# Gated attention and a SiLU layer on one core: the fourth pair's first product in plain fp32, spare tiles for the first chunks, a new order

## The chip, the cores and the metric

The kernel runs on one core of one Trainium2 chip. The core has a matmul engine (PE, with its weight loads listed apart as PEld), a vector engine (DVE), an activation engine (ACT), GpSimd (POOL) and SyncE (SP); the last two serve here mostly to issue DMAs. The metric is the device time of one execution in microseconds (us). Before the change the median of 3 runs was 649.08 us (647.99 to 651.11).

## The reference

The program computes a gated linear attention step by step over 768 positions, for 4 batches and 8 heads of 48 channels, and passes its output through a two-matrix layer with a SiLU between. `x` has 3072 rows (tokens) of 384 values, `w_in` is 384 x 2048, `w_out` 2048 x 384.

```
mag = sqrt(a_re^2 + a_im^2);  scale = min(mag, 0.999) / (mag + 1e-6)
for t in range(768):
    S_re, S_im = (ar*S_re - ai*S_im + k_t v_t^T,  ar*S_im + ai*S_re)
    y[t] = q_t . S_re
x = y as (3072, 384)
h = x @ w_in;   g = h * sigmoid(h);   out = g @ w_out
```

## The kernel before, in words

**Tiling.** The 3072 tokens are cut into 24 chunks of 128, and two chunks make a pair of 256 tokens (12 pairs, 0 to 11). For a chunk `n` the attention part turns the gates into log decays (`l`, tile `s1`) and angles (`th`), sums them along the chunk with a matmul (`L`, `phase`), takes exponentials and sines (`eq`, `ek`, `cs`), multiplies them into q and k (`qr`, `kr`), transposes these (`T`), forms the weights of the chunk (`a`, masked into `w`), and multiplies by v and by the carried state (`y`). The pair's output stands transposed in `xT`.

**The layer.** For a pair `p` and a step `jp` of 0 to 7 (256 hidden columns each), `hidden` (token `h:p.jp`) makes the first product into a PSUM tile `h`, `silu` (`g:p.jp`) applies the activation, and `result` (`r:p.jp`) adds the second product into `o`. There are two PSUM tiles for `h`.

**Plain and in parts.** A product is either plain (fp32 operands, line 755: 6 products of 128x128 by 128x256 for a step, which the trace shows as 12 matmuls) or in parts (fp32r operands, line 762: three forms, coarse, fine and diff, 18 matmuls for a step). Which pair does what is in the table `IN_PARTS`: pairs 0 to 2 are plain, 3 to 11 in parts. The parts of x are `xH` (ACT), `xL` and `xD` (DVE), two tiles of each, used by odd and even pairs in turn. The parts of `w_in` are made once, for each of the eight steps, by `v_head` (ACT, line 796), `v_tail` (DVE, 800), `v_scaled` (ACT, 804) and `v_placed` (ACT, 810), which overwrites the plain weights in place, so it has to follow the last plain product of those columns. The fine part is written to DRAM (`vk`) and read back for each use (`lv`) into a ring of three tiles that the second product's `diff` loads share; `v_mixed` (`vx`, DVE) makes the third form from it, once for pair 3 and from pair 4 on once for two pairs. The second product is in parts from pair 2 on.

**What sets the order.** The program is a list of some 1900 tokens; each issues one such step on its engines, and each engine works through its instructions in that order. Tiles are taken from rings, so a step also waits until the tile's former reader is done. DMAs are issued from SP and POOL (the token's letter `g` means POOL), from ACT for the output. Tokens `warm:n` are `n` matmuls without use.

Of the kernel before, what the change touches and what calls it, by code (L numbers as in the profile page):

```python
# [70 lines left out]
def kernel(  # L71
# [985 lines left out]
    with tc.manual_schedule():  # L1057
        for x in """
                re:0 im:0 e0:0 e1:0 warm:30 e2:0 im:1 e4:0 re:1g e0:1 e6:0 e7:0 e1:1 e2:1 warm:34
                e3:0 e5:0 re:2g e8:0 e4:1 e6:1 im:2g L:0 e3:1 exp:0 im:3g q:0g e5:1 e7:1 at:0.0  # L1060
                re:3g e8:1 an:0.0 at:0.1 k:0g L:1 dk:0 an:0.1 phase:0 G0:1 phase:1 k:1g rd:0 dq:0
                v:0g rd:1 turn:0 q:1g trig:0 turn:1 trig:1 F: G5:1 warm:20 F: rq:0.0 exp:1 rk:0.0
                hold: last:0 G8:1 rq:0.1 rk:0.1 t:0.2 H: v:1g G1:1 k:2g t:0.3 sm:0 G7:1 q:2g T:0.3
                dq:1 dk:1 t:0.0 T:0.2 s:0 rq:1.1 G2:1 t:0.1 rk:1.1 ends:0 T:0.0 t:1.3 w:0.0 F:
                rq:1.0 G3:1 T:1.3 H: G4:1 T:0.1 G6:1 G9:1 lk:0 L:2 t:1.1 exp:2 rk:1.0 w:0.1 m:0.0
                v:2g R: m:0.1 L:3 Ga:1 S:0 thirds:0 T:1.1 s:1 phase:2 ends:1 re:4g J: q:3g sm:1
                exp:3 lk:1 dq:2 rd:2 k:3g turn:2 trig:2 S:1 H: w:1.1 F: t:1.0 t:1.2 dk:2 rk:2.0
                T:1.0 rk:2.1 T:1.2 y:0 last:2 t:2.0 R: im:4g T:2.0 thirds:2 x:0 m:1.1 w:1.0 F:
                phase:3 H: R: F: thirds:1 m:1.0 rd:3 turn:3 re:5g rq:2.0 trig:3 t:2.1 rq:2.1 y:1 R:
                im:5g J: x:1 t:2.2 J: R: R: dk:3 G0:2 J: s:2 t:2.3 h:0.1 H: H: dq:3 ends:2 last:1  # L1070
                T:2.2 rq:3.1 rk:3.1 rk:3.0 F: v:3g rq:3.0 T:2.1 J: h:0.0 H: R: G5:2 w:2.0 S:2 t:3.0
                t:3.2 k:4g m:2.0 T:2.3 g:0.1 t:3.1 J: T:3.0 T:3.2 g:0.0 q:4g w:2.1 m:2.1 J: t:3.3
                w:3.0 G1:2 ends:3 last:3 y:2 m:3.0 F: G7:2 T:3.1 H: T:3.3 F: r:0.0 w:3.1 x:2 F: H:
                R: G3:2 thirds:3 R: G6:2 F: F: J: G8:2 G2:2 m:3.1 r:0.1 k:5g G9:2 y:3 H: R: H: R:
                F: im:6g v:4g F: x:3 s:3 J: Ga:2 R: H: h:1.0 J: R: h:1.1 sm:2 F: im:7g F: carried:5
                H: G4:2 L:4 g:1.0 carried:4 J: S:3 r:1.0 h:1.2 H: g:1.1 J: r:1.1 exp:4 g:1.2 F: R:
                phase:4 R: H: F: ends:4 lk:2 h:0.2 J: re:6g J: rd:4 h:0.3 R: R: turn:4 H: trig:4
                last:4 H: dq:4 r:1.2 F: F: re:7g F: phase:5 g:0.2 J: R: J: R: Q:4 h:1.3 dk:4 H:
                rd:5 J: K:4 turn:5 g:0.3 R: H: L:5 H: J: R: F: g:1.3 exp:5 J: R: r:0.2 G0:3 q:5g F:
                H: F: s:4 H: v:5g J: H: r:1.3 R: tk:4 h:1.4 g:1.4 ends:5 F: J: R: trig:5 J: F: F:  # L1080
                h:0.4 h:0.5 tq:4 H: dk:5 F: J: G5:3 g:0.4 H: G1:3 G7:3 r:0.3 J: r:1.4 R: G8:3 h:1.5
                dq:5 g:0.5 R: Q:5 H: td:4 r:0.4 G3:3 H: J: S:4 R: R: K:5 r:0.5 G2:3 H: w:4.1 J: J:
                J: tk:5 tq:5 g:1.5 G4:3 G6:3 q:6g w:4.0 wq:0 G9:3 k:6g m:4.1 wd:0 h:0.6 q:7g ws:0
                v:6g wq:1 td:5 im:8g Ga:3 m:4.0 wd:1 wq:3 g:0.6 L:6 wk:0 ws:1 wq:7 wd:3 exp:6 h:0.7
                wq:2 we:0 y:4 wq:4 r:0.6 wq:5 carried:6 dk:6 x:4 wd:2 carried:7 g:0.7 ws:2 w:5.0
                m:5.0 v:7g wk:1 re:8g last:5 wq:6 ends:6 w:5.1 ws:3 we:1 m:5.1 phase:6 rd:6 dq:6
                wd:5 im:9g we:3 h:1.6 k:7g turn:6 y:5 L:7 r:1.5 wk:2 wd:4 we:5 wk:3 ws:5 we:2 g:1.6
                trig:6 ws:4 x:5 s:5 q:8 Q:6 k:8 wd:7 S:5 re:9g K:6 xd:2 wk:5 r:1.6 we:4 ws:7 exp:7
                tk:6 tq:6 vh:1 h:1.7 h:2.0 wk:4 wd:6 we:7 last:6 g:1.7 phase:7 v:8 h:2.1 wk:7 vh:0
                rd:7 g:2.0 vt:1 vt:0 gr:2.0 r:1.7 vs:1 vs:0 r:0.7 turn:7 td:6 vp:0 w:6.0 vp:1 vk:1  # L1090
                of:1 gb:2.0 G0:4 w:6.1 ws:6 m:6.0 we:6 g:2.1 m:6.1 of:0 vk:0 G5:4 dk:7 G1:4 y:6
                lw:2.1 s:6 wk:6 G2:4 gc:2.0 G7:4 G3:4 G8:4 ends:7 h:2.2 G4:4 dq:7 lw:2.0 G6:4 r:2.0
                gr:2.1 k:9 lw:2.2 h:2.4 ss:6 vh:2 q:9 G9:4 g:2.2 sm:3 gb:2.1 gc:2.1 Ga:4 r:2.1 vt:2
                x:6 gr:2.2 v:9 vh:3 trig:7 lk:3 sd:6 gb:2.2 vt:3 gc:2.2 vs:2 re:10 h:2.3 r:2.2 hl:8
                last:7 ul:8 g:2.3 L:8 g:2.4 h:2.5 vs:3 Q:7 K:7 im:10 carried:8 exp:8 ht:8 tk:7 vk:2
                tq:7 h:2.6 ut:8 lw:2.3 gr:2.3 im:11 gb:2.3 gc:2.3 vp:2 g:2.5 phase:8 vk:3 ends:8
                lw:2.4 vh:5 vp:3 vt:5 td:7 r:2.3 gr:2.4 vh:4 hl:9 gb:2.4 vt:4 g:2.6 dk:8 rd:8 h:2.7
                s:7 vp:4 re:11 vp:5 vs:5 vh:7 dq:8 vh:6 ul:9 turn:8 S:6 gc:2.4 r:2.4 vk:5 ss:7
                last:8 carried:9 vs:4 w:7.1 vt:7 trig:8 q:10 gr:2.5 w:7.0 vt:6 vs:7 g:2.7 vk:4 K:8
                vs:6 m:7.1 L:9 Q:8 exp:9 vk:7 vp:6 m:7.0 tk:8 ht:9 dk:9 vk:6 vp:7 ut:9 lw:2.5 tq:8  # L1100
                G0:5 y:7 ends:9 gb:2.5 G5:5 gc:2.5 x:7 phase:9 r:2.5 G1:5 k:11 lw:2.6 gr:2.6 s:8
                rd:9 v:10 G8:5 G7:5 G3:5 turn:9 dq:9 gb:2.6 ss:8 G6:5 gc:2.6 G9:5 lw:2.7 r:2.6 xd:3
                Ga:5 trig:9 gr:2.7 gb:2.7 carried:10 xh:3 lv:3.0 gc:2.7 k:10 td:8 r:2.7 G2:5 xt:3
                ht:10 xg:3 vx:3.0 ut:10 G4:5 h:3.0 g:3.0 lv:3.1 im:12 phase:10 vx:3.1 hl:10 ul:10
                h:3.1 gr:3.0 gb:3.0 L:10 carried:11 sd:7 lw:3.0 g:3.1 ht:11 lv:3.2 last:9 gc:3.0
                im:13 re:12 rd:10 r:3.0 K:9 lv:3.3 Q:9 turn:10 gr:3.1 vx:3.2 re:13 gb:3.1 ut:11
                w:8.0 exp:10 m:8.0 last:10 h:3.2 phase:11 tk:9 trig:10 rd:11 tq:9 ends:10 w:8.1
                vx:3.3 dq:10 Q:10 hl:11 q:11 lw:3.1 ul:11 turn:11 lv:3.4 td:9 gc:3.1 S:7 G0:6 dk:10
                h:3.3 r:3.1 m:8.1 s:9 g:3.2 sd:8 G5:6 g:3.3 vx:3.4 ss:9 last:11 K:10 y:8 gr:3.2
                lw:3.2 gb:3.2 L:11 G1:6 tk:10 x:8 h:3.4 lv:3.5 exp:11 tq:10 lv:3.6 ends:11 gc:3.2  # L1110
                G7:6 w:9.0 r:3.2 m:9.0 G2:6 gr:3.3 vx:3.5 G3:6 G4:6 w:9.1 v:11 dk:11 m:9.1 h:3.5
                td:10 trig:11 G6:6 g:3.4 lw:3.3 dq:11 G8:6 s:10 gb:3.3 G9:6 hl:12 y:9 vx:3.6 x:9
                ss:10 gc:3.3 h:3.6 r:3.3 K:11 sd:9 gr:3.4 Q:11 w:10.1 Ga:6 tk:11 w:10.0 g:3.6 ul:12
                g:3.5 lw:3.4 gb:3.4 gc:3.4 tq:11 sm:5 m:10.1 lw:3.5 carried:12 m:10.0 r:3.4 gr:3.5
                L:12 y:10 gb:3.5 sm:4 ht:12 exp:12 ut:12 xd:4 gc:3.5 r:3.5 lv:3.7 td:11 carried:13
                S:8 x:10 lk:4 lk:5 gr:3.6 k:12 vx:3.7 phase:12 xh:4 lw:3.6 h:3.7 S:9 lv:4.0 rd:12
# [260 lines left out]
```

## Time and profile before

| | |
|---|---|
| median of 3 runs | 649.08 us (647.99 to 651.11) |
| the profiled execution | 648.07 us |
| its span, first to last instruction | 646.3 us |
| PE busy | 604.0 us (93%) |
| DVE busy | 493.9 us (76%) |
| ACT busy | 461.7 us (71%) |
| mean granted PE clock | 0.98 of 2.4 GHz |

The busy time of an engine counts overlapping instructions once. A matmul's own time is longer than its share of a dense run, because matmuls are pipelined: how fast PE goes is read from the distance between the starts of two groups. The program ends with PE at 640 us; behind it lie the last copies and the store.

### The profile page before, as it was taken

The numbers are of one execution on the slowest core, as the hardware profiler recorded it, in microseconds if no ns is written. First come the engines' busy times: TensorE is split into PE (matmuls) and PEld (weight loads), VectorE is DVE, ScalarE is ACT, GpSimd is POOL, SyncE is SP. The second block draws the span as 40 slices with busy tenths as digits, with TensorE's granted clock in tenths as the row PEclk, the third lists the DMA queues.
The fourth block names the chain that finished last, engine by engine and source line by source line (L and its number), as shares of the span: only waits on it lengthen the run. The fifth ranks groups of instructions, "written<-read, shape, count | busy, mean of one in ns | idle before, by whom it ended". The sixth has DMA issues, their size and how long they took to land. (4 is left out here: it accounts for less than half of the span.)

```text
span 646.3 us, 12653 instructions
## 1 busy us (share of the span) xinstructions
PE 604.0 (93%) x4356; PEld 543.4 (84%) x4356; DVE 493.9 (76%) x763; ACT 461.7 (71%) x722; POOL 223.6 (35%) x389
## 2 busy tenths in 40 slices
PE   6689999999987799989999998998999999999996
...
PEclk9789999999999899979999999999999999999999
...
GB/s 184 191 97 200 228 169 225 93 205 168 208 163 185 215 214 168 223 130 251 175 154 169 181 169 166 201 161 146 190 126 205 161 177 167 142 206 193 203 197 68
DMA packets 168452, 114.27 MB, mean 177 GB/s; under 512 B 137804, under 2 KB 143504, under 8 KB 168384
## 3 DMA queue, kind: packets, MB, share of 16 engines
...
q0 software_dynamic: 12288, 17.23, 13.5%
...
## 5 line engine op out<-in xcount | busy, mean ns | idle before, releaser
L306 ACT ACT_TABLE_LOAD x73 | 93.7, 1283 | 2.8 <-ACT ot L948 1.2
L593 POOL DMA_DIRECT2D T<-sq x120 | 70.3, 611 | 65.7 <-PE o L935 26.3
L896 ACT ACTIVATE head<-g 128x512 fp32r<-128x512 f32 x75 | 47.2, 629 | 50.9 <-PE o L935 42.9
L312 ACT ACTIVATE g<-h 128x512 f32<-128x512 f32 x96 | 56.1, 592 | 37.7 <-PE h L762 32.1
L525 POOL DMA_DIRECT2D dec<-ends x48 | 30.9, 649 | 150.4 <-DMA ends<-eq 148.8
L762 PE MATMUL h<-xD,mixed 128*128 128x256 f32 x432 | 75.7, 283 | 2.4 <-DVE mixed L834 1.9
L762 PE MATMUL h<-xH,coarse 128*128 128x256 f32 x432 | 76.4, 285 | 1.3 <-ACT g L312 1.2
L762 PE MATMUL h<-xL,fine 128*128 128x256 f32 x432 | 75.3, 282 | 1.4 <-DMA fine<-w_firsts 1.4
L834 DVE SCALAR_TENSOR_TENSOR tail<-head,g 128x512 fp32r<-128x512 f32 x75 | 51.2, 683 | 29.1 <-ACT head L896 18.5
L935 PE MATMUL o<-coarse,head 128*128 128x384 f32 x300 | 68.1, 349 | 2.2 <-ACT head L896 2.2
L935 PE MATMUL o<-diff,gd 128*128 128x384 f32 x300 | 66.9, 344 | 3.3 <-DVE gd L838 3.1
L935 PE MATMUL o<-fine,tail 128*128 128x384 f32 x300 | 65.7, 341 | 2.9 <-DVE tail L834 2.9
L755 PE MATMUL h<-xT,w 128*128 128x256 f32 x288 | 65.5, 381 | 2.4 <-ACT g L312 1.5
L762 PEld LDWEIGHTS h<-xH,coarse 128*128 128x128 f32 x432 | 62.9, 188 | 3.7 <-ACT g L312 2.0
L762 PEld LDWEIGHTS h<-xD,mixed 128*128 128x128 f32 x432 | 61.6, 189 | 4.1 <-DVE mixed L834 3.2
L755 PEld LDWEIGHTS h<-xT,w 128*128 128x128 f32 x288 | 54.1, 190 | 12.4 <-ACT g L312 2.6
L762 PEld LDWEIGHTS h<-xL,fine 128*128 128x128 f32 x432 | 61.5, 188 | 1.6 <-DMA fine<-w_firsts 1.6
L935 PEld LDWEIGHTS o<-diff,gd 128*128 128x128 f32 x300 | 52.8, 189 | 7.2 <-DVE gd L838 5.5
L606 PE MATMUL a<-T 96*128 96x128 f32 x384 | 53.8, 289 | 4.2 <-DMA fine<-w_firsts 2.7
L935 PEld LDWEIGHTS o<-fine,tail 128*128 128x128 f32 x300 | 53.3, 190 | 4.9 <-DVE tail L834 4.6
L606 PEld LDWEIGHTS a<-T 96*128 96x128 f32 x384 | 51.0, 203 | 7.3 <-issue 3.0
L834 DVE SCALAR_TENSOR_TENSOR mixed<-fine,coarse 128x768 fp32r<-128x768 f32 x40 | 38.1, 952 | 24.9 <-PE h L762 13.5
...
## 6 DMA issues: line engine op xcount, KB each, us to landing
...
raw<-in_moe_w_in_dram SPq DMA_DIRECT2D x24, 192.0 KB
```

The costliest lines, as they stand in the source:

```text
L306: nc.scalar.preload_act_table_set(SETS[of][0])
L312: nc.scalar.activation(out=out, in_=in_, func=func, **kw)
L525: nc.gpsimd.dma_start(out=x["dec"][a * D:(a + 1) * D], in_=ends[n].rearrange("(h d) -> d h", d=D))
L593: (nc.gpsimd if a % 2 else nc.sync).dma_start(out=to[ts(b, Q), :, a], in_=X[n]["sq"][ts(a, Q), b].rearrange("p w h x -> p (w h) x"))
L606: nc.tensor.matmul(ps[:, h], lhsT=x["kT"][hh * HH + h], rhs=x["qT"][hh * HH + h], start=True, stop=True)
L755: nc.tensor.matmul(ps[:, ji], lhsT=of_first(w1, dc, jp * 2 + ji), rhs=A[p]["xT"][:, dc], start=(dc == 0), stop=(dc == ND - 1))
L762: nc.tensor.matmul(ps[:, ji], lhsT=w(dc, ji), rhs=x[:, dc], start=(f == 0 and dc == 0), stop=(f == len(forms) - 1 and dc == ND - 1))
L834: nc.vector.scalar_tensor_tensor(out=dst, in0=head.bitcast(F32), scalar=-FINER / MORE, in1=whole, op0=ALU.mult, op1=ALU.add)
L896: nc.scalar.mul(g_form(p, jp, "head"), A[p]["g", jp], MORE * SPLIT / FINER)
L935: nc.tensor.matmul(to, lhsT=left[:, ji, ts(m, C)], rhs=right(ji), start=(first_ and ji == 0 and n == 0), stop=(last_ and ji == 1 and n == 2))
```

## The change

Four things change. The table `IN_PARTS` makes pair 3 plain, so its `xh`, `xt`, `xg` and its eight `lv` and `vx` are gone from the list (19 tokens), and the parts of `w_in` are made during pair 3's first product, not pair 2's. The tiles `xH`, `xL` and `xD`, which nothing uses before pair 4, hold for the first four chunks the log decays (`l`), `kr` of chunks 1 and 3 and the masked weights `w` of chunks 1 and 3. `v` of chunk 3 has a tile of its own. And the whole list of tokens is in another order; two of its lines stand here.

```diff
-    IN_PARTS = (0, 0, 0, 8, 8, 8, 8, 8, 8, 8, 8, 8)
+    IN_PARTS = (0, 0, 0, 0, 8, 8, 8, 8, 8, 8, 8, 8)
...
-            X[n]["all v"] = ld.tile([C, DM + 64 - D], F32, tag="v", name=f"v{n}", bufs=3)
+            X[n]["all v"] = (su if n == 3 else ld).tile([C, DM + 64 - D], F32, tag="v", name=f"v{n}",
+                                                     bufs=1 if n == 3 else 3)
...
                 g["l"] = g[x] = flat(pre.tile([C, 2, H, D], F32, tag="s1", name=f"s1_{p}"))
+                if p < 2:
+                    g["l"] = flat(moe.tile([C, 2, H, D], F32, tag=f"xH{p}", name=f"l{p}", bufs=1))
...
-                x[w + "r"] = att.tile([C, H, 2, D], F32, tag=w + "r", name=f"{w}r{n}",
-                                     bufs=1)
+                spare = w == "k" and n in (1, 3)
+                x[w + "r"] = (moe if spare else att).tile(
+                    [C, H, 2, D], F32, tag=f"xH{n // 2}" if spare else w + "r", name=f"{w}r{n}", bufs=1)
...
-        x["w", hh] = att.tile([C, HH, C], F32, tag="w", name=f"w{n}_{hh}", bufs=2)
+        spare = n in (1, 3)
+        x["w", hh] = (moe if spare else att).tile(
+            [C, HH, C], F32, tag=f"x{'LD'[hh]}{n // 2}" if spare else "w", name=f"w{n}_{hh}",
+            bufs=1 if spare else 2)
...
-                re:0 im:0 e0:0 e1:0 warm:30 e2:0 im:1 e4:0 re:1g e0:1 e6:0 e7:0 e1:1 e2:1 warm:34
...
+                warm:34 t:0.1 lk:1 G4:1 dq:1 G3:1 t:0.2 dk:1 T:0.1 F: L:2 rk:1.1 rk:1.0 s:0 H: q:2g
```

On ACT, before, between the activations of pair 2's steps 6 and 7. `coarse1`, `v_fine` and `v_head` are the parts of `w_in`, `g2_6` is pair 2, step 6, `head2_5` the first form of the second product.

```order
L312 ACTIVATE g2_6_1934<-h2_6_1862 128x512
L312 ACTIVATE turn8_1937<-phase8_1884,round_b_110 128x384
L810 ACTIVATE coarse1_2_1955<-v_head4_1926 128x3x256
L810 ACTIVATE coarse1_2_1955<-v_head5_1894 128x3x256
L804 ACTIVATE v_fine5_1897<-v_fine5_1897 128x768
L796 ACTIVATE v_head7_1960<-w1_3_90 128x768
L796 ACTIVATE v_head6_1963<-w1_3_90 128x768
L804 ACTIVATE v_fine4_1932<-v_fine4_1932 128x768
L312 ACTIVATE cs8_1996<-turn8_1937 128x8x48 x2
L312 ACTIVATE cs8_1996<-cs8_1996,half_pi_b_108 128x8x48
L896 ACTIVATE head2_5_2002<-g2_5_1881 128x512
L804 ACTIVATE v_fine7_1994<-v_fine7_1994 128x768
```

The same place on ACT after the change, from pair 2's step 6 to behind its step 7.

```order
L313 ACTIVATE g2_6_2094<-h2_6_1981 128x512
L903 ACTIVATE head2_6_2124<-g2_6_2094 128x512
L450 CAST th_parts10_2135<-th5_1879 128x384
L313 ACTIVATE g2_7_2144<-h2_7_2097 128x512
L450 CAST l_parts10_2163<-s1_5_1877 128x384
L811 ACTIVATE v_fine1_2104<-v_fine1_2104 128x768
L313 ACTIVATE turn10_2171<-phase10_2141,round_b_110 128x384
L903 ACTIVATE head2_7_2176<-g2_7_2144 128x512
```

Of the 24 ACT instructions for the parts of `w_in` (8 of each line), 3 stand ahead of this place's end after the change (two `v_head`, one `v_fine`); before, all 24 stood ahead of pair 3's first product.

On PE, before, around the first product of pair 3 (`h3_0`); `o2` is pair 2's second product.

```order
L935 MATMUL o2_0_1708<-coarse_1276,head2_7_2159 128x384 x2
L935 MATMUL o2_1_1709<-coarse_1276,head2_7_2159 128x384 x2
L935 MATMUL o2_0_1708<-fine7_1544,tail2_7_2161 128x384 x2
L935 MATMUL o2_1_1709<-fine7_1544,tail2_7_2161 128x384 x2
L935 MATMUL o2_0_1708<-diff2_7_2133,gd2_7_2168 128x384 x2
L935 MATMUL o2_1_1709<-diff2_7_2133,gd2_7_2168 128x384 x2
L762 MATMUL h3_0_2211<-xH3_2164,coarse1_0_1599 128x256 x3
L762 MATMUL h3_0_2211<-xL3_2201,fine3_0_2166 128x256 x3
L762 MATMUL h3_0_2211<-xD3_2205,mixed3_0_2207 128x256 x3
```

On PE after the change; `h3_0` reads `xT3` and the plain weights `w1_0`.

```order
L762 MATMUL h2_7_2097<-xT2_1372,w1_3_90 128x256 x6
L610 MATMUL a8_1_2110<-T8_2038 128x128 x4
L762 MATMUL h3_0_2117<-xT3_1796,w1_0_87 128x256 x6
L466 MATMUL phase10_2141<-th_parts10_2135,upto_r_102 128x384 x2
L942 MATMUL o2_0_1698<-coarse_1295,head2_6_2124 128x384 x2
```

The first product of pair 3 has moved ahead of the last two steps of pair 2's second product, and no longer reads `xH3`, `fine3_0` or `mixed3_0`.

On SP after the change, the load of pair 4's first fine part (`fine4_0`) and what is issued ahead of it.

```order
L820 DMA w_firsts<-v_fine7_2736 128x768
L882 DMA diff3_7_2824<-w_diffs 128x768
L169 DMA re7_2838<-in_a_re_dram 128x8x48
L169 DMA im7_2845<-in_a_im_dram 128x8x48
L652 DMA xT5_2772<-y3_5_2774 16x256 x3
L824 DMA fine4_0_2883<-w_firsts 128x768
L500 DMA last<-turn12_2716 1x384
```

On SP before, the same load.

```order
L593 DMA T11_2839<-sq11_2742 32x8x64 x6
L181 DMA k12_2863<-in_k_dram 128x8x48
L875 DMA diff3_6_2872<-w_diffs 128x768
L817 DMA fine4_0_2895<-w_firsts 128x768
L169 DMA re7_2904<-in_a_re_dram 128x8x48
```

The load has moved from behind the loads for step 6 of pair 3's second product to behind those for step 7.

## Rows read from the trace of the kernel before

**Rows 1.** The page: busy time of each engine, and two lines of 40 slices
```profile
PE 604.0 (93%) x4356; PEld 543.4 (84%) x4356; DVE 493.9 (76%) x763; ACT 461.7 (71%) x722; POOL 223.6 (35%) x389
PE   6689999999987799989999998998999999999996
PEclk9789999999999899979999999999999999999999
```

**Rows 2.** Busy time by stretch: length, busy us of PE to POOL, clock, DMA, GB/s
```profile
0.00:48.00 48.00, 35.00 (x232) 25.80 (x234) 34.79 (x66) 40.99 (x66) 25.11 (x47) 0.89 0.70 157
48.00:156.00 108.00, 107.03 (x607) 83.24 (x605) 89.28 (x149) 87.44 (x131) 39.18 (x59) 1.00 0.74 186
156.00:230.00 74.00, 63.71 (x380) 53.32 (x379) 52.39 (x75) 70.48 (x104) 22.88 (x41) 0.95 0.70 188
230.00:294.00 64.00, 59.70 (x496) 55.47 (x495) 53.76 (x80) 45.76 (x75) 31.32 (x56) 0.95 0.78 189
156.00:294.00 138.00, 123.41 (x874) 108.79 (x873) 106.14 (x154) 116.24 (x178) 54.20 (x95) 0.95 0.74 189
294.00:640.00 346.00, 338.56 (x2651) 325.54 (x2649) 263.42 (x396) 216.71 (x347) 105.08 (x190) 1.00 0.68 174
```

**Rows 3.** Whom PE waited for between 156 and 294: us, times, longest
```profile
PE a L606 <- DMA fine<-w_firsts: 2.7, 1, 2.7
PE o L935 <- DVE gd L838: 2.6, 3, 1.0
```

**Rows 4.** PE in order of time: start us, us, instruction, count; plain, then parts
```profile
105.59 7.93 PE L755 MATMUL h<-xT,w 128*128 128x256 f32 x36
113.36 5.32 PE L917 MATMUL o<-w,g 128*128 128x384 f32 x16
...
575.73 0.52 PE L762 MATMUL h<-xH,coarse 128*128 128x256 f32 x3
...
577.86 0.51 PE L762 MATMUL h<-xH,coarse 128*128 128x256 f32 x3
```

**Rows 5.** Groups by line: busy us, mean ns of one, idle before
```profile
L796 ACT ACTIVATE v_head<-w 128x768 fp32r<-128x768 f32 x8 | 6.6, 839 | 0.0
L834 DVE SCALAR_TENSOR_TENSOR mixed<-fine,coarse 128x768 fp32r<-128x768 f32 x40 | 38.1, 952 | 24.9 <-PE h L762 13.5 <-DMA fine<-w_firsts 11.2
```

**Rows 6.** ACT in order of time around 201 us
```profile
200.47 1.58 ACT L810 ACTIVATE coarse<-v_head 128x768 fp32r<-128x768 f32 x2
201.94 0.84 ACT L804 ACTIVATE v_fine<-v_fine 128x768 fp32r<-128x768 f32 x1
```

**Rows 7.** PE in order of time: starts of the first products of pairs 4 and 5
```profile
288.89 0.52 PE L762 MATMUL h<-xH,coarse 128*128 128x256 f32 x3
...
294.32 0.51 PE L762 MATMUL h<-xH,coarse 128*128 128x256 f32 x3
```

**Rows 8.** SP's issue of pair 4's first fine part, in order of time
```profile
274.39 0.32 SPq L817 DMA_DIRECT2D fine<-w_firsts  x1
```

**Rows 9.** DMA issues from POOL: count, KB each, median us to landing
```profile
im<-in_a_im_dram POOLq DMA_DIRECT2D x8, 192.0 KB, 4.3
q<-in_q_dram POOLq DMA_DIRECT2D x8, 192.0 KB, 6.4
```

**Rows 10.** ACT in order of time ahead of the second half of pair 0's xT
```profile
41.70 1.28 ACT L306 ACT_TABLE_LOAD   x1
...
47.45 0.58 ACT L312 ACTIVATE turn<-phase,round_b 128x384 f32<-128x384 f32 x1
...
50.14 0.55 ACT L247 ACTIVATE r<-raw 128x384 int32<-128x384 uint32 x1
```

**Rows 11.** PE in order of time: matmuls without use, and one phase at two clocks
```profile
2.13 8.93 PE L969 MATMUL idle<-upto_r 128*128 128x256 bf16 x64 [2.13 <-POOL upto_r L283]
...
19.82 1.65 PE L460 MATMUL phase<-th,upto_r 128*128 128x384 f32 x2 [1.19 <-DVE th L433]
...
95.17 0.81 PE L460 MATMUL phase<-th,upto_r 128*128 128x384 f32 x2
```

More of the change, by code (lines that the diff above doesn't have):

```diff
@@ L1058 @@
         for x in """
-                re:0 im:0 e0:0 e1:0 warm:30 e2:0 im:1 e4:0 re:1g e0:1 e6:0 e7:0 e1:1 e2:1 warm:34
[L1060 to L1116, printed above, removed]
-                w:11.0 re:14 sd:10 turn:12 w:11.1 m:11.0 m:11.1 gb:3.6 y:11 g:3.7 im:14 x:11 ht:13
@@ L1196 @@
[L1196 to L1200 removed]
+                re:0 e0:0 im:0 re:1g e1:0 hold: im:1 q:0g e2:0 e3:0 e4:0 e5:0 e0:1 e6:0 e7:0 e1:1
@@ new lines @@
+                L:9 g:2.5 tk:8 lw:2.3 ht:9 r:2.2 gr:2.3 ut:9 gb:2.3 v:9 G0:5 sd:6 h:2.4 G5:5 w:7.1
+                last:8 lw:2.5 gc:2.3 g:2.4 Q:8 q:10 exp:9 lw:2.4 m:7.1 G1:5 sd:7 r:2.3 tq:8 dk:9
+                w:7.0 m:7.0 phase:9 rd:9 turn:9 G2:5 ends:9 S:6 h:2.6 dq:9 G7:5 G4:5 gr:2.4 gb:2.4
+                k:10 vh:1 gc:2.4 y:7 r:2.4 G3:5 G8:5 x:7 G6:5 gr:2.5 td:8 lw:2.6 G9:5 trig:9 xd:3
+                gb:2.5 gc:2.5 Ga:5 s:8 vh:0 r:2.5 g:2.6 h:2.7 vt:1 ss:8 im:12 w:8.1 Q:9 h:3.0
+                gr:2.6 K:9 v:10 tk:9 carried:10 last:9 ht:10 tq:9 ut:10 gb:2.6 phase:10 g:2.7
```

216 lines of the change are left out of this document (133 added, 83 removed).

## The prediction, made before the result was known

> **What bounds the kernel now.** I read the busy times first, then the same times cut into stretches, then PE's waits in the one stretch that stands out, then PE in order of time for the price of a product. The page [rows 1] says PE 604.0 us of 646.3, and its line of slices says where the rest is: PE is below 9 at the start and again in slices 12 to 14, and the clock line dips there too. Cut at the points where the work changes [rows 2], the reader is to see four stages. From 0 to 48 us (attention of the first chunks) ACT is the busy one, 40.99 of 48, and PE idles 13. From 48 to 156 (plain pairs 0 and 1) PE is busy 107.03 of 108. From 156 to 294 (pairs 2 and 3, in which the parts of `w_in` are made) PE is busy 123.41 of 138 at a mean granted clock of 0.95. From 294 to 640 PE is busy 338.56 of 346, which is 97.85%, at full clock. So PE bounds everywhere but at the start and between 156 and 294, and there ACT does in the first part: 70.48 of 74 us from 156 to 230, and then only 45.76 of 64. PE's waits in that stage are many small ones [rows 3], on forms made by ACT and DVE and on a DMA: the sign of helpers that are late, not of one long chain.
>
> **The change part by part.** The sum is made against the profiled execution, 648.07 us (its span of 646.3 and 1.8 around it), which is 1.0 below the median of 649.08.
>
> *Pair 3's first product, plain.* A plain step takes (113.36 - 105.59) / 3 = 2.59 us on PE, a step in parts (577.86 - 575.73) = 2.13 [rows 4]. Eight steps cost 8 x 0.46 = 3.7 us more PE. The Trainium skill, "FP8 and Floating Point Precision" (section TensorE Precision Notes), says that true FP32 takes 4 passes through the array; against three forms that would be 2.13 x 4/3 = 2.84, 8 x 0.71 = 5.7 us, and a sum 2.0 us higher. The trace disagrees by 0.25 us a step; I take the measured 3.7. Off ACT goes one `xH`, a 128x768 activation as `v_head` is (0.84 us), off DVE eight `mixed` (0.95 each) and the two of the same size for `xL` and `xD`, 9.5 together [rows 5], and off the DMA queues eight loads of 384 KB: none of that lies on the path by itself, but it thins out the stage.
>
> *The parts of `w_in`, during pair 3.* Nothing is added or removed: 24 ACT instructions of 0.84 us, which follow each other at (201.94 - 200.47) / 2 = 0.735 [rows 5, 6], so 17.6 us of ACT, leave the stretch in which ACT is 95% busy and enter the one in which it is 72% busy. The whole stage then has 116.24 - 0.84 = 115.4 us of ACT and, for PE, this: a mean clock of 0.95 between the two levels of 1.2 and 2.4 GHz is 10% of 138 us at the lower, in which 6.9 us are lost; 123.41 - 6.9 = 116.5, plus 3.7 is 120.2. If PE is as busy as from 294 on, that takes 120.2 / 0.9785 = 122.8 us where it took 138: a gain of 15.2. With no idle time at all it would be 17.8; if ACT binds it is less (first rival).
>
> *The turn to pair 4.* Here I expect a new wait. Before, `fine4_0` was issued at 274.39 and its product began at 288.89, 14.5 us later [rows 7, 8]. Now its tile is the one that step 6 of pair 3's second product frees, and on PE only a state, a phase and step 7 lie between. Before, a state and step 7 lay between the first products of pairs 4 and 5: 294.32 - 288.89 - 2.13 = 3.3 us [rows 4, 7], to which the phase adds little; I take 3.5. A load of 192 KB takes 4.3 to 6.4 us to land [rows 9]; for 384 KB I have no row, so 4.3 is the lower end and 12.8, twice the longer one, the upper. I take 6.0, as the 192 KB rows are the nearest, and add 0.95 for `mixed`: a wait of 3.5, with ends at 0 and at 10.3. Queued behind it on PE are the first products of pairs 4 and 5; ACT and DVE wait for these.
>
> *The spare tiles and the new start.* ACT sets the start. Ahead of the second half of pair 0's `xT`, ACT now has one table load (1.28 us) and chunk 3's turn and three sines fewer (50.14 - 47.45 = 2.7 us with their idle time) [rows 10], 4.0 at most. The spare tiles take waits for a tile away that I can't find as rows, so they get no price of their own. Against it, 34 of the matmuls without use now stand between chunk 0's first and second transpose, 34 x 8.93 / 64 = 4.7 us [rows 11], where PE had idled anyway. I take a gain of 2.0, with ends at 4.0 gained and 4.7 lost. Since PE is 99% busy right behind, what is gained there stays.
>
> *From 294 us on.* PE issues the same matmuls. The order differs, so the 7.4 us that PE idles there could vanish or double; I take 0, and 7 to either side.
>
> Sum: -15.2 + 3.5 - 2.0 = -13.7, so 634.4 for the profiled execution and 635 for the median.
>
> **The rivals.**
> *ACT binds in the fourth pair.* The moved work comes with the work already there: 45.76 + 17.6 - 0.84 = 62.5 us of ACT from 230 to 294, where PE needs 59.7 - 3.2 + 3.7 = 60.2. At the 95% share that ACT reached [rows 2] that is 65.7 us, and the stretch from 156 to 230 takes (63.71 - 3.7) / 0.9785 = 61.3: together 127, a gain of 11.0 where I put 15.2, so 639.6, 640. (3.7 and 3.2 are what the lower clock loses in each stretch, worked out as above.) For it: the two sums are close. Against it: the new order also moves pair 3's first product ahead of pair 2's last steps, so PE has work in hand.
> *The start gets worse.* The useless matmuls delay the transposes by their full 4.7 us: -15.2 + 3.5 + 4.7 = -7.0, so 642. The clock tells for it: a phase took 1.65 us at 19.82, near a wait, and 0.81 later [rows 11], at granted clocks that average 0.89 in the first 48 us and 1.00 behind [rows 2]. Two phases at the lower clock cost 2 x 0.84 = 1.7 us, which is inside this rival. The Trainium skill, "TensorE: Matmul & The Clock Gate" (What's actually happening), says the default state is throttled and activity releases it; by that, the first sums, ahead of which no matmul stands now, run at 1.2 GHz, and the trace agrees so far as PE at the start shows both levels. Against it: ACT, not PE, is the busy one there.
> *Slower: the reload of the fine parts becomes the loop of pairs 4 and 5.* The ring of three tiles now carries, close together, the parts' writing, pair 3's `diff` loads and pair 4's `fine` loads. If each of the eight `fine` loads waits as the first does, 8 x 3.5 = 28 us are lost, and -15.2 - 2.0 + 28 = +10.8: 659, as a median 660. It decides from 17.2 / 8 = 2.2 us a load. For it: the first load is late by its place. Against it: each part then serves two pairs, 4 x 2.1 us of PE, which is longer than a landing of 6.4 and 0.95; and the same loop ran at 97.85% behind 294 [rows 2].
>
> **How the numbers follow.** The forecast gets 0.63 (635, its own range 627 to 643), ACT binding 0.20 (640), the worse start 0.08 (642), the reload 0.07 (660), the rest 0.02. The terms' ends reach from 648.07 - 17.8 - 4.0 - 4 (half of the late idle gone) = 622 to about 650; that they fall together is unlikely. The range 626 to 646 leaves out the reload and little else. What a measurement of this kernel can tell is about 0.5%, 3.2 us: faster is below 645.8. That holds for nearly all of the first three cases, 0.86; 0.06 for no change; 0.08 for slower.
>
> **What would show it.** Right: PE at 97% or more and clock 1.00 between pair 2's start and pair 3's end; ACT no longer at 95% before pair 3; pair 4's first product beginning some 13 us earlier than 288.89; one wait of 2 to 6 us for `fine` or `mixed` right before it. Wrong: ACT at 95% during pair 3 with PE waiting for `head` (first rival); pair 0's first product no earlier than before, and PE between 48 and 156 as full (second); repeated waits of `h` for `fine` or `mixed` in pairs 4 and 5 (third); or a PE share from pair 4 on that falls below 97%, which I hold constant without a reason beyond equal work.

## The result, and the profile after

| | before | changed |
|---|---|---|
| median, range | 649.78 us (647.99 to 651.11) | 619.01 us (618.46 to 619.32) |
| ratio, 95% interval | | 0.9527 (0.9501 to 0.9554) |
| the profiled execution | 648.07 us | 619.32 us |
| its span | 646.3 us | 617.6 us |

The kernel became about 31 us faster. The forecast was 635 (626 to 646): the sign was right, the gain more than twice the 14 us forecast, and the time lies below the range.

First the page after, against [rows 1]: busy times, and the lines of 40 slices for PE and its clock.

```profile
span 617.6 us, 12518 instructions
PE 593.4 (96%) x4308; PEld 538.2 (87%) x4308; DVE 486.6 (79%) x753; ACT 455.9 (74%) x717; POOL 220.7 (36%) x389
PE   3899999999999999999999999999999999999996
PEclk9899999999999999999999999999999999999999
```

The dip of slices 12 to 14 is gone from both lines, as forecast. PE has fewer busy us than before although its work grew; that is a point to come back to. The same by stretch, against [rows 2] (length, busy us of PE to POOL, granted clock, DMA, GB/s).

```profile
0.00:48.00 48.00, 35.23 (x267) 27.43 (x268) 38.24 (x74) 42.23 (x70) 26.96 (x51) 0.96 0.80 187
48.00:156.00 108.00, 107.79 (x583) 82.76 (x583) 90.11 (x147) 88.14 (x133) 40.78 (x63) 1.00 0.76 184
156.00:230.00 74.00, 73.45 (x493) 65.18 (x492) 58.17 (x86) 65.18 (x104) 32.22 (x57) 1.00 0.75 179
230.00:294.00 64.00, 60.76 (x473) 56.01 (x471) 55.17 (x79) 59.61 (x88) 25.79 (x47) 1.00 0.83 209
156.00:294.00 138.00, 134.21 (x964) 121.18 (x962) 113.34 (x165) 124.79 (x191) 58.01 (x104) 1.00 0.79 193
276.00:611.00 335.00, 331.06 (x2618) 321.49 (x2618) 258.24 (x386) 217.07 (x345) 99.82 (x180) 1.00 0.69 175
```

Between 156 and 294 PE issues 964 matmuls where it issued 874, at clock 1.00 where it was 0.95. ACT is down from 95% to 88% before 230 and up from 72% to 93% behind. Whom PE waits for, from 156 to 276, against [rows 3], is now two rows.

```profile
PE h L762 <- ACT g L313: 1.7, 2, 1.2
PE h L769 <- DVE mixed L841: 1.0, 1, 1.0
```

**A measure that can be compared.** Busy time can't be, since a matmul at half clock is busy twice as long. So every matmul got one price, the mean distance from its start to the next start, by kind, over the fastest nine tenths in the changed kernel: 0.213 us in a plain first product, 0.118 in one in parts, 0.174 in a second product in parts, and so on. Cutting the kinds another way moves a whole column, the first by some 10 us, but the differences between its rows by no more than half a us: only these are read. Elapsed time less the prices of what PE had issued is what was lost, to waits, to the lower clock, to filling up again. All matmuls together cost 551.4 us before and 554.8 now. The loss by stretch, the stretches ending at the activations named:

| kernel | to pair 1's last | to pair 3's first | to pair 4's first | to pair 11's last |
|---|---|---|---|---|
| before | 33.0 | 19.2 | 11.9 | 23.4 |
| changed | 29.2 | 3.9 | 6.8 | 17.9 |
| e1_plain_alone | 33.2 | 12.2 | 44.8 | 28.1 |
| e2_old_homes | 32.8 | 4.6 | 7.3 | 17.2 |
| e3_late_old | 29.6 | 4.1 | 6.8 | 35.3 |
| e5_start_old | 33.6 | 15.1 | 6.6 | 17.3 |
| e7_more_act | 30.9 | 4.9 | 11.3 | 17.7 |
| e8_new_order_parts | 29.9 | 37.7 | 26.1 | 17.6 |
| e9_no_idle34 | 34.5 | 4.1 | 7.2 | 17.5 |
| e10_start_alone | 29.4 | 18.1 | 7.6 | 23.5 |
| e11_late_old | 29.3 | 4.1 | 6.6 | 21.2 |
| e12_scaled_on_dve | 29.1 | 4.1 | 6.7 | 17.7 |
| e13_layer_new | 34.2 | 14.6 | 51.7 | 25.3 |
| e14_layer_old | 28.9 | 16.4 | 30.8 | 17.6 |

Of the change, 3.8 us come from the start, 20.4 from pairs 2 and 3, 5.5 from pair 4's first activation to pair 11's last, and 2.4 behind that; 3.4 of added work go off. That is the 28.7 between the two profiled spans.

### The profile page after: what moved, and what is told of

The parts are those of the page before. It is cut to its first block, busy times and chain, and to the rows that moved or that the text cites. A ratio compares the mean times of both kernels' runs of the same rounds, so it can differ in the third digit from the quotient of the medians.

```text
span 617.6 us, 12518 instructions
## 1 busy us (share of the span) xinstructions
PE 593.4 (96%) x4308; PEld 538.2 (87%) x4308; DVE 486.6 (79%) x753; ACT 455.9 (74%) x717; POOL 220.7 (36%) x389
## 4 chain that ended last, share of the span: by engine, by line
PE 72%; ACT 14%; issue 3%; DMA 3%; DVE 3%; SPq 1%; POOL 1%; ACTq 0%; DVEq 0%; POOLq 0%
PE o L942 22%; PE h L769 20%; PE h L762 9%; PE o L924 6%; PE a L610 5%; ACT L307 3%; ACT s L313 3%; PE y L640 3%; ACT mag L313 3%; PE y L643 2%; ACT g L313 1%; PE s L711 1%; DMA re<-in_a_re_dram 1%; DMA T<-sq 1%; PE phase L466 1%
## 5 line engine op out<-in xcount | busy, mean ns | idle before, releaser
L762 PE MATMUL h<-xT,w 128*128 128x256 f32 x384 | 87.9, 381 | 1.9 <-ACT g L313 1.7
L762 PEld LDWEIGHTS h<-xT,w 128*128 128x128 f32 x384 | 72.0, 190 | 13.7 <-ACT g L313 2.4
L841 DVE SCALAR_TENSOR_TENSOR tail<-head,g 128x512 fp32r<-128x512 f32 x75 | 51.4, 685 | 36.5 <-ACT head L903 19.3
L528 POOL DMA_DIRECT2D dec<-ends x48 | 30.9, 648 | 119.7 <-DMA ends<-eq 113.3
L769 PE MATMUL h<-xH,coarse 128*128 128x256 f32 x384 | 67.6, 284 | 1.7 <-ACT g L313 1.7
L769 PE MATMUL h<-xD,mixed 128*128 128x256 f32 x384 | 66.9, 282 | 1.4 <-DVE mixed L841 1.0
L769 PE MATMUL h<-xL,fine 128*128 128x256 f32 x384 | 67.0, 283 | 0.0
L769 PEld LDWEIGHTS h<-xH,coarse 128*128 128x128 f32 x384 | 55.7, 188 | 3.7 <-ACT g L313 2.7
L769 PEld LDWEIGHTS h<-xD,mixed 128*128 128x128 f32 x384 | 54.8, 189 | 2.2 <-DVE mixed L841 1.2
L769 PEld LDWEIGHTS h<-xL,fine 128*128 128x128 f32 x384 | 54.7, 188 | 0.1
L845 DVE SCALAR_TENSOR_TENSOR gd<-tail,g 128x512 fp32r<-128x512 f32 x75 | 51.4, 686 | 3.7
L942 PEld LDWEIGHTS o<-coarse,head 128*128 128x128 f32 x300 | 50.4, 188 | 3.7 <-ACT ot L955 1.4
```

Of the source, the lines that this page charges most:

```text
L528: nc.gpsimd.dma_start(out=x["dec"][a * D:(a + 1) * D], in_=ends[n].rearrange("(h d) -> d h", d=D))
L762: nc.tensor.matmul(ps[:, ji], lhsT=of_first(w1, dc, jp * 2 + ji), rhs=A[p]["xT"][:, dc], start=(dc == 0), stop=(dc == ND - 1))
L769: nc.tensor.matmul(ps[:, ji], lhsT=w(dc, ji), rhs=x[:, dc], start=(f == 0 and dc == 0), stop=(f == len(forms) - 1 and dc == ND - 1))
L841: nc.vector.scalar_tensor_tensor(out=dst, in0=head.bitcast(F32), scalar=-FINER / MORE, in1=whole, op0=ALU.mult, op1=ALU.add)
L845: nc.vector.scalar_tensor_tensor(out=dst, in0=tail.bitcast(F32), scalar=MORE / FINER, in1=whole, op0=ALU.mult, op1=ALU.subtract)
L942: nc.tensor.matmul(to, lhsT=left[:, ji, ts(m, C)], rhs=right(ji), start=(first_ and ji == 0 and n == 0), stop=(last_ and ji == 1 and n == 2))
```

## The experiments

Two lists of tokens were joined or mixed in most of them. Where a mixed list took a tile before its former reader had been issued, the step was put off until it could be.

**Each part by itself.** The move of the weights' parts alone, in the old order (e1; some steps put off):

```diff
-    IN_PARTS = (0, 0, 0, 8, 8, 8, 8, 8, 8, 8, 8, 8)
+    IN_PARTS = (0, 0, 0, 0, 8, 8, 8, 8, 8, 8, 8, 8)
-   tk:6 tq:6 vh:1 h:1.7 h:2.0 ... lv:3.0 ... vx:3.0 ut:10 G4:5 h:3.0 g:3.0
+   tk:6 tq:6 h:1.7 h:2.0 ... ut:10 G4:5 h:3.0 vh:1 g:3.0
```

> The kernel before with one part of the change alone: pair 3's first product plain, and the making of the parts of w_in moved, step for step, from pair 2's activations to pair 3's. Order of all else and all tiles as before. Theory (relief): between 156 and 294 us ACT starved PE, and the product matmuls and the rest of that stage are only about 112 us of real work, so the relief alone, in the old order, gives at least half of the stage's 19 us: 633 to 641, and ACT no longer at 95% before pair 3. Rival (order): the stage is fast only because the new order keeps PE work in hand; the relief alone moves the same waits one pair later: 647 to 655.

Measured: 676.57 us (674.08 to 680.63), ratio 1.0417 (1.0378 to 1.0457): 28 us slower than before. Its stage by stretch:

```profile
156.00:230.00 74.00, 67.25 (x398) 56.59 (x397) 46.70 (x69) 59.32 (x88) 25.98 (x45) 0.98 0.55 134
230.00:294.00 64.00, 51.25 (x332) 44.63 (x330) 40.37 (x60) 45.17 (x69) 26.04 (x46) 0.87 0.59 137
```

ACT is down to 59.32 of the first 74 us, and the part up to pair 3's first activation loses 7 us less than before (12.2 for 19.2). But pair 3 then loses 44.8 for 11.9, with ACT idle for 19 of 64 us. PE's largest waits from 150 to 330 us are for loads and for DVE, and ACT's `head` comes behind them with 1.6:

```profile
PE o L935 <- DMA diff<-w_diffs: 6.7, 1, 6.7
PE o L935 <- DVE tail L834: 5.0, 4, 3.0
PE o L935 <- DVE gd L838: 5.0, 4, 2.9
PE h L762 <- DMA fine<-w_firsts: 4.6, 1, 4.6
```

So it is not ACT's load that holds pair 3 here. Both theories put the time too low, mine by more.

The opposite, the new order with pair 3 still in parts (e8; some steps put off):

```diff
-    IN_PARTS = (0, 0, 0, 0, 8, 8, 8, 8, 8, 8, 8, 8)
+    IN_PARTS = (0, 0, 0, 8, 8, 8, 8, 8, 8, 8, 8, 8)
-   g:1.7 w:6.0 G4:4 ... gb:2.4 k:10 vh:1 gc:2.4 ... Q:9 h:3.0
+   g:1.7 w:6.0 G4:4 vh:1 vt:1 vs:1 ... gb:2.4 k:10 gc:2.4 ... lv:3.0 vx:3.0 h:3.0
```

> The changed kernel's order and tiles, but pair 3 in parts as before: the steps that make the parts of w_in stand at pair 2's steps, and pair 3's own parts, reloads and mixed forms stand ahead of its products. Theory (order and place belong together): between 156 and 210 us ACT would need 45.8 + 17.6 + 0.8 = 64 us of 54, so 10 us or more are lost and 3.4 saved: 626 to 650. Rival (the new order alone makes the gain, plain pair 3 only costs 3.4): 613 to 620.

Measured: 671.51 us (669.45 to 673.66), ratio 1.0355 (1.0320 to 1.0389), above both expectations. PE's waits between 156 and 296, the largest:

```profile
PE h L769 <- DMA fine<-w_firsts: 11.7, 2, 9.5
PE h L769 <- ACT g L313: 6.1, 1, 6.1
PE a L610 <- DVE turn L482: 4.0, 1, 4.0
```

The order alone makes no gain either. Of the four combinations, the two mixed ones lose 58 and 52 us against the changed kernel, and 28 and 21 against the old one. A mixed list is not tuned, so these numbers are no price of either part; they show that neither part makes the gain without the other, as far as such lists can tell.

**The layer's steps or the attention's?** The new sequence of first products, forms and second products of pairs 2 to 4, in the old surroundings of e1 (e13; 7 put off), and the old sequence in the changed kernel (e14; 11 put off). Shown are first (h) and second (r) products alone:

```diff
 e14, against the changed kernel:
-   h:2.4 r:2.3 h:2.6 r:2.4 r:2.5 h:2.7 h:3.0 r:2.6 h:3.1 r:2.7 h:3.3
+   h:2.5 h:2.6 r:2.3 h:2.7 r:2.4 r:2.5 r:2.6 r:2.7 h:3.0 h:3.1 r:3.0
```

> The old order and old tiles with pair 3 plain and the parts of w_in made at pair 3's steps (676.6 us in the first experiment), but the layer's steps of pairs 2 to 4 (first product, activation, forms, reload and second product) in the new sequence among themselves; the attention's steps and the making of the parts keep their old places, seven steps stand later where a tile asks for it. Theory (the layer's sequence keeps PE's work in hand: first products stand further ahead of second products): 660 or less. Rival (the attention's steps around them carry the gain): 668 or more.

> The changed kernel with the layer's steps of pairs 2 to 4 in the old sequence among themselves; everything else keeps its new place, eleven steps stand later where a tile asks for it. Theory (the layer's sequence): 640 or more, with waits of PE for forms between 190 and 260 us. Rival (the attention's steps carry it): 628 or less.

Measured: 689.12 us (686.15 to 690.11) and 654.81 us (653.57 to 657.08). The theory holds for e14 and falls for e13. In the changed kernel, putting the layer's steps of pairs 2 to 4 back into the old sequence, in which pair 3's first product stands behind pair 2's second, costs 36 us. PE's largest waits between 156 and 296 in e14, and its stretch from 210 to 276:

```profile
PE o L942 <- ACT head L903: 5.2, 2, 2.8
PE y L640 <- DVE ssq L718: 5.0, 1, 5.0
PE o L942 <- DVE tail L841: 3.5, 1, 3.5
```

```profile
210.00:276.00 66.00, 53.48 (x292) 46.69 (x293) 39.46 (x59) 42.46 (x64) 23.78 (x42) 0.80 0.59 141
```

PE waits for `head` and `tail` of the very step it is at: with no first product in between, activation and forms are on its path. That the new sequence alone doesn't help (e13) says that it needs other steps around it; which of these, the runs don't tell. In e13 `h:3.0` also stands one second product later than in the changed kernel, so it lacks the new sequence just at the turn to pair 3, and like e14 it is a mixed list.

**How much ACT decides.** The kernel before without the eight `v_scaled` (e4); the changed kernel with each of them doubled (e7); the changed kernel with their scale done on DVE (e12).

```diff
 e4, in the kernel before, v_scaled:
-        nc.scalar.mul(V["fine", jp], V["fine", jp].bitcast(F32), MORE / FINER)
+        return
 e7, in the changed kernel, v_scaled:
+        nc.scalar.mul(V["fine", jp], V["fine", jp].bitcast(F32), 1.0)
         nc.scalar.mul(V["fine", jp], V["fine", jp].bitcast(F32), MORE / FINER)
 e12, in the changed kernel, v_head, v_tail, v_scaled, v_placed:
-        nc.scalar.mul(V["head", jp].bitcast(F32R), first_of(w1, jp), SPLIT)
+        nc.scalar.mul(V["head", jp].bitcast(F32R), first_of(w1, jp), SPLIT / FINER)
-        nc.vector.tensor_tensor(out=V["fine", jp], in0=first_of(w1, jp), in1=V["head", jp],
-                                op=ALU.subtract)
+        nc.vector.scalar_tensor_tensor(out=V["fine", jp], in0=first_of(w1, jp), scalar=1 / FINER,
+                                       in1=V["head", jp], op0=ALU.mult, op1=ALU.subtract)
-        nc.scalar.mul(V["fine", jp], V["fine", jp].bitcast(F32), MORE / FINER)
+        return
-        nc.scalar.mul(first_of(V["coarse"], jp), V["head", jp], FINER)
+        nc.scalar.mul(first_of(V["coarse"], jp), V["head", jp], FINER * FINER)
```

> The kernel before, in its own order, without the eight v_scaled (the fine parts stay unscaled, so the first product of pairs 3 to 11 is wrong): 8 x 0.735 = 5.9 us of ACT less in the stretch in which ACT is 95% busy, nothing moved, PE's work the same. Theory (ACT's throughput is what PE waits for between 156 and 230 us): 5 to 8 us faster, 640 to 643. Rival (the waits are those of a list in which PE's next product stands behind late forms, whatever ACT's load): at most 2 faster, 646 to 648.

> The changed kernel with every v_scaled preceded by one more activation of the same tile by 1.0: 8 x 0.735 = 5.9 us more of ACT between 210 and 276 us, where ACT is busy 62.1 of 66 us and PE 63.9. Theory (the new order keeps PE's work in hand, but ACT is within 4 us of the bound there): 2 to 4 us slower, 621 to 623. First rival of the prediction (ACT already binds): 5 to 7 slower, 624 to 626. No bound at all: 618 to 620.

> The changed kernel with 5.9 us of ACT taken off between 210 and 276 us: the scale of the fine parts goes into v_tail on DVE (the head is made 4096 times as large, and the eight v_scaled are gone; the factor 1 + 2^-12 of the fine parts with them). Theory (ACT binds there, as the added activations showed, but PE is right behind it with 2.2 us of idle time and some filling): 2 to 4 us faster than the changed kernel, 615 to 617. Rival (DVE, or PE itself, binds at once): 618 to 620.

Measured: e4 645.92 us (641.47 to 648.13), ratio 0.9920 (0.9882 to 0.9959), so 5.2 us (2.7 to 7.7) for the 5.9 taken off. The gain is the theory's lower edge and the interval leaves out the rival's 2, but the median itself stands at the rival's 646, as the runs of the kernel before beside it had a median of 650.10. Its profiled run was the slowest of its five, so its stretches aren't read. e7 624.99 us (623.62 to 626.50), 6.0 more than the changed kernel for 5.9 of added ACT: the first rival's figure. e12 619.40 us (618.73 to 620.43): no gain, the rival's figure. The stretch from 210 to 276 in the changed kernel, and then in e7:

```profile
210.00:276.00 66.00, 63.85 (x479) 57.61 (x478) 56.05 (x83) 62.10 (x99) 27.47 (x51) 1.00 0.84 212
```

```profile
210.00:276.00 66.00, 60.80 (x446) 53.73 (x445) 50.71 (x76) 63.82 (x100) 25.66 (x48) 1.00 0.75 182
```

ACT was busy 94% there and can take little more; PE falls from 479 matmuls to 446. Less ACT work helps nothing, as the stretch from 156 to 294 of e12 shows against the one of the changed kernel above: ACT 5.5 us lower, PE the same to the matmul.

```profile
156.00:294.00 138.00, 134.34 (x964) 121.28 (x962) 113.54 (x165) 119.25 (x183) 58.68 (x105) 1.00 0.80 193
```

The changed stage is balanced: PE at 97% and ACT at 94% at once.

**The start.** The changed kernel with the old tiles (e2; 7 steps put off); the old order up to 158 us with the rest new (e5; 1 put off); the new start alone on the kernel before (e10; none); the changed kernel without 34 of the matmuls without use (e9).

```diff
 e2, homes of l, kr, w and v as before the change, and
-   F: L:2 rk:1.1 rk:1.0 s:0 H: q:2g
+   F: L:2 s:0 rk:1.1 rk:1.0 H: q:2g
 e5, behind the old list's g:1.7 all that is left in the new order
-   g:2.0 g:1.7 w:6.0 G4:4 G6:4 turn:7
+   we:7 last:6 g:1.7 phase:7 G0:4 G5:4 G1:4
 e10, behind the new list's x:5 all that is left in the old order
     IN_PARTS = (0, 0, 0, 8, 8, 8, 8, 8, 8, 8, 8, 8)
-   we:3 wd:5 r:0.6 k:8 x:5 we:5 phase:7 wd:7
+   we:3 wd:5 r:0.6 k:8 x:5 v:7g we:5 ws:5 g:1.6
 e9
-   rq:0.1 lk:0 k:2g warm:34 t:0.1 lk:1
+   rq:0.1 lk:0 k:2g t:0.1 lk:1
```

> The changed kernel's order and its plain pair 3, but l, kr, w and v of the first four chunks back in the tiles of before; seven steps stand later in the list, where a tile would otherwise be taken before its reader (both halves of kr of chunks 1 and 3, one transpose of chunk 3, both masked weights of chunk 1). Theory: the spare tiles serve the start only, and the start gained 2 to 3 us: 619 to 623. Rival (spare tiles make the start's pipeline, and the old tiles make chunk 1 wait for chunk 0's last readers): 627 or more, with new waits of DVE for PE before 48 us.

> The old order up to the end of pair 1's first product (at 158 us), then all that is left in the changed kernel's order, with the changed kernel's tiles throughout. Theory: the start gained 2 to 3 us and the stages behind keep theirs: 620 to 623. Rival: the new start also leaves the layer's steps in a better place for pair 2 (preparation of pair 2's attention and of the second product's parts done earlier), and the stage from 156 us loses with it: 627 or more.

> The start of the change alone: its order and its spare tiles up to chunk 5's xT (at about 150 us), then all that is left in the old order, pair 3 in parts. At that point the two orders have issued nearly the same steps, so nothing has to be moved at the joint. Theory (the start is worth 3.8 us by itself, and PE is full behind it): 645 to 646. Rival (what the start gains is lost in the wait-bound stage behind 156 us, which waits for ACT and not for PE): within 1 us of the kernel before, 648 to 651.

> The changed kernel without the 34 matmuls without use between chunk 0's first and second transpose. The forecast: PE idles there anyway, so no change, 618 to 620. The second rival's price: they delay the transposes by up to 4.7 us, so 614 to 617 without them. A third way: they hold the granted clock up for what follows, so without them 1 us or more slower, 620 to 623.

Measured: e2 623.09 us (622.70 to 624.08), just above the theory's upper end; e5 637.60 (637.00 to 637.97), on its rival's side of 627; e10 639.00 (638.09 to 641.53), ratio 0.9842 (0.9805 to 0.9879); e9 620.65 (620.42 to 621.35).

The first column of the table makes a square of e2 and e5: old order and old tiles 33.0, old order with new tiles 33.6, new order with old tiles 32.8, both new 29.2. Only both together gain, and the spare tiles carry all of it in the new order: 3.6 us at pair 1's end, 4.1 at the end of the kernel. e5's joint loses 11 us more in pair 2 (15.1 for 3.9); that steps which the new order has done by then come all at once there is likely, but not shown. Its later columns equal the changed kernel's.

e10 was expected at 645 to 646 and gained 11.3 us by the medians, 9.1 in the profiled span. The start gave 3.6 of these; most of the rest is one place. PE in the kernel before, around the turn to pair 4 [rows 7], with its wait of 2.7 us [rows 3], and then the same passage in e10:

```profile
270.00:276.00 6.00, 6.00 (x60) 5.79 (x60) 5.87 (x11) 5.70 (x10) 4.95 (x9) 1.00 0.81 170
276.00:282.00 6.00, 3.32 (x19) 3.14 (x18) 0.54 (x2) 1.23 (x2) 2.77 (x6) 0.74 0.82 199
282.00:288.00 6.00, 6.00 (x48) 5.59 (x47) 4.40 (x7) 1.44 (x4) 0.62 (x2) 0.69 0.17 33
288.00:294.00 6.00, 6.00 (x52) 5.52 (x51) 3.99 (x7) 4.59 (x9) 1.23 (x3) 1.00 0.82 214
```

```profile
258.00:264.00 6.00, 5.21 (x36) 4.92 (x35) 5.53 (x8) 3.30 (x5) 4.37 (x8) 1.00 0.89 273
264.00:270.00 6.00, 6.00 (x54) 5.20 (x53) 5.23 (x11) 3.97 (x9) 5.02 (x9) 1.00 0.94 206
270.00:276.00 6.00, 5.41 (x49) 4.96 (x49) 3.69 (x8) 3.18 (x5) 2.69 (x5) 1.00 0.96 231
```

Before, PE is busy 3.32 of 6 us, and the clock is 0.74 in that stretch and 0.69 in the next, in which PE is busy all 6.00 us. What the clock keeps back there is 0.26 x 6 + 0.31 x 6 = 3.4 us at most, as PE still waited in the first part of it. In e10 the two waits there are 0.8 and 0.6 and the clock stays at 1.00. From pair 3's last activation to pair 4's first the loss is 6.3 us before and 1.5 in e10: one wait of 2.7 had cost more than itself.

What PE waited for there is not what [rows 3] name. `a` reads `T` and no fine part:

```profile
278.92 0.55 POOL L722 DMA_DIRECT2D S<-ssq  x1 [0.31 <-DMA T<-sq]
279.54 3.75 PE L606 MATMUL a<-T 96*128 96x128 f32 x16 [2.68 <-DMA fine<-w_firsts]
```

The load of the fine part, issued at 274.39 [rows 8], shares a completion semaphore with one of the twelve loads of `T`, and its completions were still coming in; hence the name. By the trace's completion records the last load of `T`, issued by POOL at 273.99, landed at 279.13, 0.4 us before `a` began. In e10 `a` waits in the same way, once under the name of `diff` (0.8) and once under that of `T` (0.6). Why these loads were less late in e10 is not shown.

e9 is the third way. It has 34 matmuls less and is 1.6 us slower; the two kernels' ranges don't overlap, but they weren't run side by side. PE from 20 to 40 us in the changed kernel, and in e9:

```profile
20.00:40.00 20.00, 19.17 (x156) 16.25 (x154) 18.57 (x33) 19.21 (x32) 9.36 (x13) 0.95 0.72 179
```

```profile
20.00:40.00 20.00, 16.96 (x108) 14.46 (x107) 17.54 (x32) 17.75 (x29) 7.97 (x11) 0.77 0.69 177
```

The clock falls from 0.95 to 0.77. In order of time, first the changed kernel, then e9:

```profile
24.26 3.87 PE L976 MATMUL idle<-upto_r 128*128 128x256 bf16 x34
27.97 0.60 PE L579 MATMUL tp<-ident,kr 128*96 128x128 f32 x4
36.89 0.91 PE L463 MATMUL phase<-th,upto_r 128*128 128x384 f32 x2 [0.54 <-DVE th L436]
```

```profile
26.33 0.64 PE L579 MATMUL tp<-ident,kr 128*96 128x128 f32 x4 [1.77 <-DVE kr L555]
38.59 0.81 PE L463 MATMUL phase<-th,upto_r 128*128 128x384 f32 x2
```

The 34 take 3.9 us and delay the transpose by 1.6 us, and 9 us later the kernel that has them is 1.7 us ahead. The Trainium skill, "TensorE: Matmul & The Clock Gate" (What's actually happening), says that the default is the throttled state and that activity releases it; both places agree, and the matmuls without use are worth their time here.

**The late part.** The new list up to pair 5's first activation, the rest old (e3; 10 put off), and the same with the joint at a point at which both lists have issued nearly the same steps (e11; none put off):

```diff
 e3
-   G5:7 gr:4.0 g:5.0 G1:7 gb:4.0 L:13 gc:4.0
+   G5:7 gr:4.0 g:5.0 turn:13 L:13 vx:4.1 h:4.1
 e11
-   w:13.1 G3:8 lv:4.6 hl:16 m:13.1 r:4.4 m:13.0
+   w:13.1 G3:8 k:16 h:4.5 lv:4.6 g:5.5 m:13.1
```

> The changed kernel up to pair 5's first activation (at 276 us), and behind it all that is left in the old order (ten steps around pair 4's second step later than there). Theory: of the 30 us, 6 to 8 were gained behind 294 us by the new order of the late part alone, so this gives 624 to 627. Rival: the late gain comes from what the earlier part left ready (attention chunks further ahead): 618 to 621.

> The changed kernel with only its late part in the old order: from a point at about 320 us, between the first products of pairs 4 and 5 and those of pairs 6 and 7, where both orders have issued nearly the same steps, so that nothing has to be moved at the joint. Theory (the late order is worth 4 to 5 us by itself): 622 to 625. Rival (the 17 us that the other late splice lost are the true price of the old late order): 630 or more. Second rival (the late gain is only what the earlier stages left ready): 619 to 620.

Measured: e3 640.36 us (638.55 to 642.48), outside both expectations: the joint cost most of it (19.0 us between pair 4's first activation and its last, for 6.3 in the changed kernel). e11 623.68 us (623.53 to 624.68): 4.7 us for the old late order, as the theory had it. PE's waits between 320 and 612 in e11, the longest:

```profile
PE h L769 <- DVE mixed L841: 1.6, 2, 1.1
PE h L769 <- ACT g L313: 1.2, 2, 1.0
PE h L769 <- DMA fine<-w_firsts: 0.4, 1, 0.4
```

and all of them in the changed kernel:

```profile
PE o L942 <- ACT ot L955: 1.2, 1, 1.2
PE h L769 <- DVE xD L845: 0.4, 1, 0.4
PE h L769 <- ACT g L313: 0.3, 1, 0.3
```

The table agrees. The last column is 17.2 to 17.9 in the eight kernels with the new late order, whatever stands ahead, and 21.2 to 28.1 in the five that have the old one without e3's joint.

## Why the prediction was wrong

By its own terms, on the profiled executions:

| term | forecast | measured |
|---|---|---|
| pair 3 plain | +3.7 | +3.4 |
| the stage without its losses | -18.9 | -21.4 |
| a new wait at the turn to pair 4 | +3.5 | +1.0 |
| the start | -2.0 | -3.8 |
| from pair 4 on | 0 | -7.9 |
| sum | -13.7 | -28.7 |

The forecast's -15.2 for the stage holds the 3.7 of the plain product, so it is -18.9 of loss. The measured -21.4 is the 20.4 of the table and the 1.0 of the wait inside it.

**The step that failed most** is "PE issues the same matmuls. The order differs, so the 7.4 us that PE idles there could vanish or double; I take 0". A centre of 0 was no reading of the trace but the lack of one: that equal work keeps its losses had no reason behind it, and the runs show that the order of this part decides them. Half of the miss of 15.0 lies here, 7.9 us; e11 measures 4.7 of it directly, as the price of the old order behind 320 us. Where the other 3 come from, the order between pair 4's start and 320 us or what the earlier stages left ready, stays open. The end I gave the term, 7 us to either side, fell just short.

**The stage: the size nearly right, the reason half right.** ACT's load is a price there in the kernel before (e4: 5.2 us for 5.9, 2.7 to 7.7), as the prediction read from 70.48 of 74 us. But "leave the stretch in which ACT is 95% busy and enter the one in which it is 72% busy" was priced as if the move alone did it. e1 does the move alone and loses 28 us. What the runs point to instead is the list as a whole, in which PE has a first product in hand while ACT and DVE make the forms of the second: e14 takes that away, loses 36 and has PE waiting 8.7 us for `head` and `tail`. It is not shown to be the only cause, as e14 is a mixed list and e13, with nearly the new sequence of the layer but the old surroundings, gains nothing. Taking PE's share from 294 us on for the new stage came near the truth (97.85% taken, 134.21 of 138, 97.3%, measured), for a reason that I hadn't shown.

**The turn to pair 4.** The wait came, but of 0.98 us. SP and PE there, in order of time (start us, us, engine, line, instruction, count):

```profile
266.62 0.53 SPq L824 DMA_DIRECT2D fine<-w_firsts  x1
```

```profile
269.59 0.51 PE L769 MATMUL h<-xH,coarse 128*128 128x256 f32 x3
270.00 0.62 PE L769 MATMUL h<-xL,fine 128*128 128x256 f32 x3
271.60 0.62 PE L769 MATMUL h<-xD,mixed 128*128 128x256 f32 x3 [0.98 <-DVE mixed L841]
```

The load is issued 3.0 us ahead of the product, where I took 3.5, and its first reader starts 3.4 us after the issue. I had taken 6.0 for the landing, from loads of 192 KB that POOL issues [rows 9], and even my lower end, 4.3, was too long here: this is the mis-sized part of the term. Those rows were of another queue and another shape, and the trace had better ones: by its completion records the 40 loads of this kind in the kernel before landed 2.8 to 6.6 us after their issue, median 3.7, and pair 4's first was the slowest of them. By my own working a landing of 4.3 also makes a wait of 4.3 + 0.95 - 3.5 = 1.8, not the 0 that I gave as the lower end. The rest of the wait is DVE's order. The load was in by 270.00, when PE read it, and `mixed` still had to wait its turn on DVE:

```profile
270.13 0.55 DVE L456 TENSOR_TENSOR l_parts<-s,l_parts 128x384 fp32r<-128x384 f32 x1
270.60 0.95 DVE L841 SCALAR_TENSOR_TENSOR mixed<-fine,coarse 128x768 fp32r<-128x768 f32 x1
```

The product begins 19.3 us earlier than the 288.89 of [rows 7], where 13 was forecast.

**The start.** The spare tiles "get no price of their own", since no row showed their waits; in the new order they are worth 3.6 us, nearly the whole term. The 34 matmuls without use, priced at nothing or a loss of 4.7, delay a transpose by 1.6 us and hold the clock, a net gain.

**The rivals.** ACT binding: right that it is at its bound (e7), wrong on the time. Its 95% share came out as 94%, but with PE at 97% in the same stretch. The worse start and the reload loop did not come: PE's waits in the changed kernel hold none for `fine`, and one of 1.0 us for `mixed`. The range left out the case that the terms' ends fall together, 622 by the text, and the measured time lies below even that. All four uncertain terms missed on the same side. A likely reason, not tested as such, is that one thing sets them all: the late part, the start, the wait and the stage belong to the same new list, so their errors should not have been taken as independent.
